# Moving early transfers, MLP steps, weight sums and transposes in a fused attention and MLP kernel

## The chip, the cores and the metric

The kernel runs on one core of one Trainium2 chip. Its time is the device time of one execution in microseconds (us). Three runs of the kernel before gave 350.06, 349.75 and 347.81 us, median 349.75.

## The reference

Eight batches of eight heads, 576 tokens, head size 64: forgetting attention, and then an MLP over all 4608 tokens.

```python
scores = q @ k.T / sqrt(64)
cum = cumsum(log(clip(f, 0.0001, 1.0)))
scores = where(causal, -1e9, scores + cum[i] - cum[j])
x = softmax(scores) @ v              # heads side by side: 4608 x 512
h = x @ w_in                         # 512 x 2048
out = (h - tanh(h)) @ w_out          # 2048 x 512, float32
```

## The kernel before, in words

**Slots.** The attention works on pairs of heads: four pairs in each batch, 32 pairs. Slot p makes the scores of pair p and the values (the product with v) of pair p - 1. From slot 5 on a slot is a list made by `att_items` (L559): seven score tiles, numbered 0 to 6 here. A tile is TensorE work (`scores`, L346), an exponential on ScalarE (L362) and a triangular select on GpSimd (L373). After tile 1 come `values` of the pair before (30 small matmuls on TensorE, L383, then three VectorE instructions up to L391) and `turn`, two transposing DMAs on SyncE's queue (L404, L406). For batches 0 to 2 a slot also transposes q and k of the next pair on TensorE (`trans`, L293; copied out by VectorE, L303, or in slots 7 and 8 by ScalarE, L301): behind tiles 0 and 3, in slot 5 behind tiles 2 and 4, in slots 7 and 9 behind tiles 1 and 4. The loads of later batches are hung on tiles too (`LOADS`); they follow the select of their tile in GpSimd's queue. The five loads of batch 2's v stand on tiles 2 to 6 of slot 6, the first loads of its q and k on tiles 1 to 4 of slot 5.

**MLP steps.** Between attention items a slot hands out `take` MLP steps. A block of 512 tokens has 30 steps: sixteen times `mlp1` (four matmuls, tanh on ScalarE, an addition on VectorE, L431), then fourteen half products with `w_out`, eight matmuls each. The products use Strassen's scheme, so they also need sums of the activations (`sums`, L445) and of the weights. Each quarter of the weight sums is made once, by two VectorE instructions (`wsum`, L275), which follow two neighbouring steps of block 0. With the steps counted from 0, slot 4 does steps 0 to 4; slots 5 to 8 take 6 each and slot 9 takes 7, so slot 9 ends with step 35. The products are, in this order: (1) steps 16, 17; (2) 18; (6) 19, 20; (2) 21; (5) 22, 23; (7) 24, 25; (3) 26, 27; (4) 28, 29. Product 6 needs weight sum 2, product 5 sum 0, product 7 sum 1, product 4 sum 3. Steps 21, 25, 27 and 29 close a quarter of the output and store it; two buffers `ost` hold what is being stored.

**Loads.** All loads of q, k, v and weights are issued by GpSimd, one after another, on one queue. Before, batch 0's v comes in seven DMAs: head 0, head 1, the last 64 tokens of all heads, then (after q and k of heads 6 and 7) four blocks of 128 tokens with heads 2 to 7. Batch 1, `w_in` and `w_out` follow, and batch 2's first q.

Of the kernel before, what the change touches and what calls it, by code (L numbers as in the profile page):

```python
# [17 lines left out]
FAR = 3  # L18
# [5 lines left out]
def kernel(  # L24
# [13 lines left out]
    B, H, S, D = q.shape  # L38
# [4 lines left out]
    NPAIR = H // 2  # L43
    NJ = 5
# [3 lines left out]
    NFT = DFF // P  # L48
# [31 lines left out]
    qn, kn = ([t[0:S // NT6, :].rearrange("p (h n d) -> p h n d", h=H, n=NT6) for t in raw] for raw in (qraw, kraw))  # L80
    qb, kb = ([t[:, 0:NJ * DM].rearrange("p (n e) -> p n e", n=NJ) for t in raw] for raw in (qraw, kraw))
    vn = [qkp.tile([P, NJ, H, VW], FP16, tag=f"vn{i}", name=f"vn{i}") for i in range(2)]
    QT = [qkp.tile([D + 3, H, S], FP16, tag=f"QT{i}", name=f"QT{i}") for i in range(2)]
    KT = [qkp.tile([D + 3, H, PITCH], FP16, tag=f"KT{i}", name=f"KT{i}") for i in range(2)]
# [3 lines left out]
    def load_qk(dst, src, b, h0, h1):  # L88
        nc.gpsimd.dma_start(
            out=dst[b % 2][:, h0:h1, :, :].rearrange("p h n d -> p (h n) d"),  # L90
            in_=src[b, h0:h1, :, :].rearrange("h s d -> (h s) d").rearrange("(m p) d -> p m d", p=S // NT6))
# [13 lines left out]
    def load_v_rest(b):  # L105
        nc.gpsimd.dma_start(out=vn[b % 2][0:S % P, NJ - 1, :, 0:D],
                            in_=v[b, :, S - S % P:S, :].rearrange("h p d -> p h d"))

    def load_v_head(b, h):
        nc.gpsimd.dma_start(out=vn[b % 2][:, 0:NJ - 1, h, 0:D],  # L110
                            in_=v[b, h, 0:S - S % P, :].rearrange("(n p) d -> p n d", p=P))

    def load_v_block(b, n, h0, h1):
        nc.gpsimd.dma_start(out=vn[b % 2][:, n, h0:h1, 0:D],  # L114
                            in_=v[b, h0:h1, n * P:(n + 1) * P, :].rearrange("h p d -> p h d"))

    def load_v(b):
        for n in range(NJ - 1):
            load_v_block(b, n, 0, H)
        load_v_rest(b)  # L120
# [63 lines left out]
    def cum_q():  # L184
        nc.scalar.activation(out=cq, in_=cum, func=AF.Copy, bias=-SHIFT * inv_qscale, scale=inv_qscale)

    load_v_head(0, 0)
    load_v_head(0, 1)
    load_v_rest(0)
    load_qk(qn, q, 0, 6, H)  # L190
    load_qk(kn, k, 0, 6, H)
    for n in range(NJ - 1):
        load_v_block(0, n, 2, H)

    def pads():
        nc.vector.scalar_tensor_tensor(out=pick[:, 2:3], in0=id16[:, 1:2], scalar=-1.0, in1=id16[:, NH + 1:NH + 2],
# [80 lines left out]
    def spin(n):  # L277
        t32 = ps_av.tile([P, 2, UW], FP32, tag="av", name="spin")
        for _ in range(n):
            nc.tensor.matmul(out=t32[:, 0, :], lhsT=ones16[:, 0:P], rhs=ones16[:, 0:UW])  # L280
# [7 lines left out]
    def trans(b, c, src, dst, engs):  # L288
        pn, g3 = S // NT6, NT6 // 2
        t16 = t_bank().bitcast(FP16)[:, 0:2 * S // 2].rearrange("p (a g n) -> p a g n", a=2, g=g3)  # L290
        for a in range(2):
            for g in range(g3):
                nc.tensor.transpose(out=t16[:, a, g, :], in_=src[b % 2][:, 2 * c + a, 2 * g:2 * g + 2, :],  # L293
                                    identity=id16[0:pn, 0:pn])
        for a0, an in ((0, 1), (1, 1)) if len(engs) > 2 else ((0, 2),):
            for e in range(2):
                h0 = 2 * c + a0
                to = dst[b % 2][0:D, h0:h0 + an, 0:S].rearrange("d a (g e p) -> d a g e p", g=g3, e=2)[:, :, :, e, :]
                of = t16[e * D:(e + 1) * D, a0:a0 + an, :, :]
                if engs[2 * a0 + e] == "A":  # L300
                    nc.scalar.activation(out=to, in_=of, func=AF.Copy)  # L301
                else:
                    nc.vector.tensor_copy(out=to, in_=of)  # L303
            if a0 == 0 and engs == "AAAA":
                cum_q()
# [70 lines left out]
    def values(b, c, a):  # L376
        if a == 0:
            av = ps_av.tile([P, 2, 512], FP32, tag="av", name="av")
            AV[(b, c)] = av[:, :, 0:NJ * (D + 1)].rearrange("p a (i d) -> p a i d", i=NJ)
        av = AV[(b, c)]  # L380
        for ib in range(NJ):
            for j in range(ib + 1):
                nc.tensor.matmul(out=av[:, a, ib, :], lhsT=E.pop((b, c, a, j, ib)),  # L383
                                 rhs=vn[b % 2][:, j, 2 * c + a, 0:D + 1], start=(j == 0), stop=(j == ib))
        if a == 0:
            return
        xn = XN[(b, c)] = fin.tile([P, NJ, P], FP16, tag="xn", name="xn")
        rs = fin.tile([P, 2, NJ, 1], FP32, tag="rs", name="rs")
        nc.vector.tensor_scalar_add(out=rs, in0=av[:, :, :, D:D + 1], scalar1=1e-9)  # L389
        nc.vector.reciprocal(out=rs, in_=rs)  # L390
        nc.vector.tensor_tensor(out=xn.rearrange("p i (a d) -> p a i d", a=2), in0=av[:, :, :, 0:D],  # L391
                                in1=rs.to_broadcast([P, 2, NJ, D]), op=ALU.mult)

    def turn(b, c):
        xn = XN.pop((b, c))
        r0 = b % 3 * S
        if b == 0:
            xt = t_bank().bitcast(FP16)[:, 0:S]
            for ib in (NJ - 1, 0, 1, 2, 3):
                w0 = min(ib * P, S - P)  # L400
                nc.tensor.transpose(out=xt[:, w0:w0 + P], in_=xn[:, ib, :], identity=id16)
            nc.vector.tensor_copy(out=XR[:, c, r0:r0 + S], in_=xt)
            return
        nc.sync.dma_start_transpose(out=XR[:, c, r0:r0 + S - D].rearrange("p (n t) -> p n t", t=P),  # L404
                                    in_=xn[:, 0:NJ - 1, :].rearrange("p n d -> p (n d)"))
        nc.sync.dma_start_transpose(out=XR[:, c, r0 + S - D:r0 + S], in_=xn[D:P, NJ - 1, :])  # L406
# [97 lines left out]
    for u in range(NU):  # L504
        mlp += [[(mlp1, u, ft)] for ft in (turns if u else turns[:10] + turns[12:14] + turns[10:12] + turns[14:])]
        mlp += [[(product, u, n, g)] for n, g in ((1, 0), (1, 1), (2, 0), (6, 0), (6, 1), (2, 1))]
        mlp += [[(product, u, n, g)] for n in (5, 7, 3, 4) for g in range(2)]
    for at, n in ((NFT - 2, 0), (NFT, 2), (NFT + 3, 1), (NFT + 6, 3)):
        for o in range(2):
            mlp[at + o] += [(wsum, n, o * K2 // 2, (o + 1) * K2 // 2)]  # L510

# [2 lines left out]
    def step():  # L514
        for fn, *args in mlp[STEPS[0]]:
            fn(*args)
        STEPS[0] += 1
# [7 lines left out]
    def first_slot(p):  # L525
        here = pairs[p]
        before = pairs[p - 1] if p else None
        for what in FIRST[p]:
# [27 lines left out]
            else:  # L556
                spin(int(what))

    def att_items(p):  # L559
        items = []  # L560
        before = pairs[p - 1]
        after = pairs[p + 1] if p + 1 < len(pairs) else None
        for ti in range(len(TILES)):
            if p < len(pairs):
                items.append((lambda ti=ti: scores(*pairs[p], (ti,), "late"), True))
            items += [(load, False) for load in LOADS.get((p, ti), ())]
            if after and after[0] < FAR and ti in ((1, 4) if p in (2 * NPAIR - 1, 2 * NPAIR + 1) else (2, 4) if p == NPAIR + 1 else (0, 3)):
                dst, src = (KT, kn) if ti > 2 else (QT, qn)
                items.append((lambda dst=dst, src=src: trans(*after, src, dst, "AA" if 2 * NPAIR - 1 <= p <= 2 * NPAIR else "VV"), True))
            if ti == 1:  # L570
                items += [(lambda a=a: values(*before, a), a == 1) for a in range(2)]
                items.append((lambda: turn(*before), True))
        return items

    with tc.manual_schedule(engines={PE, mybir.EngineType.Pool, mybir.EngineType.SP, mybir.EngineType.DVE,
                                     mybir.EngineType.Activation}):
        with tc.tile_pool(name="ps_t2", bufs=1, space=PSUM) as POOLS["t"]:
            with tc.tile_pool(name="ps_two", bufs=2, space=PSUM) as POOLS["s"]:
                for p in range(NPAIR):
                    first_slot(p)  # L580
        del POOLS["t"]
        POOLS["m"] = ctx.enter_context(tc.tile_pool(name="ps_m", bufs=3, space=PSUM))
        POOLS["s"] = ctx.enter_context(tc.tile_pool(name="ps_sc", bufs=2, space=PSUM))
        first_slot(NPAIR)
        for p in range(NPAIR + 1, len(pairs) + 1):
            items = att_items(p)
            take = 6 if p <= 2 * NPAIR else 7 if p == 2 * NPAIR + 1 or p % 2 == 0 else 8
            whole, given, n = sum(c for _, c in items), 0, 0
            for emit, counts in items:
                emit()  # L590
                n += counts
                while given < take and (given + 1) * whole <= n * take and STEPS[0] < len(mlp):
                    step()
                    given += 1
        while STEPS[0] < len(mlp):
            step()
# [28 lines left out]
```

## Time and profile before

| what | us |
|---|---|
| median of three runs | 349.75 |
| the profiled execution | 351.51 |
| its span | 349.7 |
| TensorE busy | 334.1 |
| VectorE busy | 253.0 |
| ScalarE busy | 220.4 |
| GpSimd busy | 179.3 |

The span runs from the first to the last instruction of the profiled execution. Busy time is the union of an engine's instructions; matmuls overlap each other, and a busy TensorE is not TensorE at its peak. "PEclk" is the granted clock of TensorE, 1.00 being full speed. An idle time of an engine counts only where that engine sets the end.

### The profile page before, as it was taken

How to read it: one execution, taken by the hardware profiler on the slowest of the kernel's cores; microseconds unless marked ns; L12 is line 12 of the kernel's file. 1: busy time of each engine (PE TensorE's matmuls, PEld its weight loads, DVE VectorE, ACT ScalarE, POOL GpSimd, SP SyncE). 2: the span in 40 equal slices, each digit the busy share in tenths (PEclk: the TensorE clock that was granted, in tenths of full speed). 3: DMA queues.
4: the chain of work that ended last, by engine and by line, in shares of the span. 5: the costliest groups of instructions: out<-in, count | busy, mean ns of one | idle time of the engine just before them, and what ended most of it. 6: DMA issues, size and time to landing. Idle time of an engine off the chain costs nothing.

```text
span 349.7 us, 8656 instructions
## 1 busy us (share of the span) xinstructions
PE 334.1 (96%) x3297; PEld 233.6 (67%) x3297; DVE 253.0 (72%) x521; ACT 220.4 (63%) x412; POOL 179.3 (51%) x327
## 2 busy tenths in 40 slices
PE   7889995997999999999999999999999999999996
PEld 2676564783568656887887568755887787477475
DVE  7686996628997489848884889378937873873872
ACT  6676873766765687568755875588558843623631
POOL 8996755484676736775567447752322220500500
PEclk9999997899999999999999999999999999999999
DMA  9999999999999997999699969994122004003003
GB/s 99 137 156 171 187 199 132 132 106 169 127 142 114 170 164 75 119 164 168 69 114 149 194 78 102 157 170 78 48 79 50 19 21 134 0 3 120 3 0 122
DMA packets 169592, 38.82 MB, mean 111 GB/s; under 512 B 155938, under 2 KB 169486, under 8 KB 169550
## 3 DMA queue, kind: packets, MB, share of 16 engines
q0 software_dynamic: 116608, 18.36, 83.9%
q1 hardware_dynamic: 52942, 19.90, 28.2%
q8 instruction: 26, 0.43, 0.5%
q14 instruction: 16, 0.13, 0.1%
HBM read 36.85 MB, written 9.44 MB: 132 GB/s over the span
## 4 chain that ended last, share of the span: by engine, by line
PE 81%; DMA 8%; DVE 6%; ACT 2%; SPq 1%; issue 1%; POOL 0%; DVEq 0%; POOLq 0%
PE mb L418 30%; PE px L466 16%; PE mb L466 14%; PE ps L346 11%; PE av L383 8%; DMA qn<-in_q_dram 6%; DMA out_dram<-ost 2%; DVE gt L431 1%; PE t L293 1%; DVE KT L303 1%; DMA ws<-in_f_dram 1%; ACT e L362 1%; DVE sm L445 1%; DVE xn L391 1%; ACT th L425 1%
## 5 line engine op out<-in xcount | busy, mean ns | idle before, releaser
L418 PE MATMUL mb<-XR,win 128*128 128x512 f16 (+4 forms) x704 | 141.3, 340 | 2.3 <-DVE gt L431 2.2
L362 ACT ACTIVATE e<-ps 128x512 f16<-128x512 f32 (+1 forms) x183 | 109.4, 618 | 23.5 <-PE ps L346 15.7
L425 ACT ACTIVATE th<-mb 128x512 f32<-128x512 f32 x144 | 86.5, 601 | 51.4 <-PE mb L418 45.8
L431 DVE TENSOR_TENSOR gt<-mb,th 128x512 f16<-128x512 f32 x144 | 97.4, 687 | 24.1 <-ACT th L425 22.7
L373 POOL TENSOR_SCALAR_AFFINE_SELECT e<-e 128x128 f16<-128x128 f16 x162 | 59.6, 372 | 99.3 <-ACT e L362 98.5
L418 PEld LDWEIGHTS <-win 128*128 128x128 f16 x704 | 61.7, 97 | 51.0 <-issue 4.4
L346 PE MATMUL ps<-QT,KT 67*128 67x448 f16 (+4 forms) x376 | 73.9, 279 | 3.1 <-DVE KT L303 1.9
L466 PEld LDWEIGHTS <-gt 128*128 128x128 f16 x576 | 54.1, 98 | 11.3 <-DVE gt L431 1.0
L346 PEld LDWEIGHTS <-KT 67*128 67x128 f16 x384 | 36.4, 98 | 25.9 <-DVE KT L303 3.8
L466 PEld LDWEIGHTS <-sm 128*128 128x128 f16 x432 | 40.9, 98 | 6.7
L496 DVE TENSOR_TENSOR ost<-mb,part 128x512 f32<-128x512 f32 x25 | 17.2, 686 | 28.2 <-PE mb L466 9.2
L466 PE MATMUL mb<-ws,gt 128*128 128x256 f16 x288 | 36.4, 272 | 0.0
L383 PEld LDWEIGHTS <-e 128*128 128x128 f16 x896 | 32.5, 98 | 3.4 <-DVE xn L391 0.6
L383 PE MATMUL av<-vn,e 128*128 128x65 f16 x896 | 34.3, 194 | 0.4 <-DVE xn L391 0.4
L483 ACT ACTIVATE part<-px 128x512 f32<-128x512 f32 x24 | 14.3, 597 | 30.2 <-PE px L466 30.2
L466 PE MATMUL px<-ws,sm 128*128 128x256 f16 x256 | 31.6, 272 | 0.0
L114 POOL DMA_DIRECT2D vn<-in_v_dram x32 | 28.4, 890 | 4.1 <-DMA wout<-in_moe_w_out_dram 2.4
L391 DVE TENSOR_TENSOR xn<-av,rs 128x640 f16<-128x640 f32 x32 | 26.4, 825 | 1.1
L389 DVE TENSOR_SCALAR rs<-av 128x10 f32<-128x10 f32 x32 | 5.2, 162 | 25.0 <-PE av L383 24.9
L445 POOL TENSOR_TENSOR sm<-gt 128x512 f16<-128x512 f16 x4 | 4.6, 1156 | 36.2 <-DVE gt L431 36.2
L95 POOL DMA_DIRECT2D qn<-in_q_dram x25 | 21.9, 875 | 1.5 <-issue 1.4
L466 PE MATMUL mb<-wout,gt 128*128 128x256 f16 x160 | 22.2, 280 | 0.0
(92 smaller groups left out, 320.4 us busy)
## 6 DMA issues: line engine op xcount, KB each, us to landing
out_dram<-ost SPq DMA_DIRECT2D x34, 256.0 KB
vn<-in_v_dram POOLq DMA_DIRECT2D x28, 128.0 KB, 5.8
qn<-in_q_dram POOLq DMA_DIRECT2D x20, 128.0 KB, 3.7
kn<-in_k_dram POOLq DMA_DIRECT2D x20, 128.0 KB, 4.3
win<-in_moe_w_in_dram POOLq DMA_DIRECT2D x4, 512.0 KB, 9.0
wout<-in_moe_w_out_dram POOLq DMA_DIRECT2D x2, 1024.0 KB, 17.1
qn<-in_q_dram POOLq DMA_DIRECT2D x10, 144.0 KB, 6.5
kn<-in_k_dram POOLq DMA_DIRECT2D x10, 144.0 KB, 6.8
```

Source lines behind the costliest of these rows:

```text
L95: nc.gpsimd.dma_start(out=dst[b % 2][0:pn, n, :].rearrange("p (h d) -> p h d", h=H), in_=src[b, :, n * P:n * P + pn, :].rearrange("h p d - ...
L114: nc.gpsimd.dma_start(out=vn[b % 2][:, n, h0:h1, 0:D], in_=v[b, h0:h1, n * P:(n + 1) * P, :].rearrange("h p d -> p h d"))
L346: nc.tensor.matmul(out=ps[:, col:col + n], lhsT=KT[b % 2][0:rows, h, j * P:(j + 1) * P], rhs=QT[b % 2][0:rows, h, i0:i0 + n], start=True, ...
L362: nc.scalar.activation(out=eb[:, :, lo:hi], in_=banks[:, 0:n2, lo:hi], func=AF.Exp, scale=qscale)
L373: nc.gpsimd.affine_select(out=view, in_=view, compare_op=ALU.is_ge, fill=0.0, base=0, pattern=pat, channel_multiplier=-1)
L383: nc.tensor.matmul(out=av[:, a, ib, :], lhsT=E.pop((b, c, a, j, ib)), rhs=vn[b % 2][:, j, 2 * c + a, 0:D + 1], start=(j == 0), stop=(j == ib))
L391: nc.vector.tensor_tensor(out=xn.rearrange("p i (a d) -> p a i d", a=2), in0=av[:, :, :, 0:D], in1=rs.to_broadcast([P, 2, NJ, D]), op=ALU. ...
L418: nc.tensor.matmul(out=hps[:, o:o + n], lhsT=win[:, ci, ft * P:(ft + 1) * P], rhs=XR[:, ci, t:t + n], start=(ci == 0), stop=(ci == NCH - 1))
L425: nc.scalar.activation(out=th, in_=hps, func=AF.Tanh, scale=-1.0)
L431: nc.vector.tensor_tensor(out=GT[(u, ft)], in0=hps, in1=th, op=ALU.add)
L466: nc.tensor.matmul(out=ps[:, g * E2:(g + 1) * E2], lhsT=left(k), rhs=right[:, k, :], start=(first and (g == 0 or last) and k == 0), stop=( ...
L496: nc.vector.tensor_tensor(out=ost, in0=ps, in1=PART.pop((u, {2: 1, 7: 5, 4: 6}[n])), op=ALU.add)
```

## The change

1. Batch 0's v is loaded by `load_v(0)`: four blocks of 128 tokens with all heads and the rest, all ahead of q and k of heads 6 and 7. That is five DMAs instead of seven.
2. Slots 5, 6 and 7 take 5 MLP steps instead of 6; slots 8 and 9 take 8 instead of 6 and 7. Slot 9 ends with step 35 as before.
3. Weight sum 2 follows steps 17 and 18 instead of 16 and 17, sum 1 steps 22 and 23 instead of 19 and 20, sum 3 steps 25 and 26 instead of 22 and 23. Sum 0 stays behind steps 14 and 15.
4. In slot 7 the transposes of q and k stand behind tiles 3 and 5 (the fourth and the sixth) instead of 1 and 4, and in slot 9 behind tiles 2 and 5 instead of 1 and 4.

```diff
-    load_v_head(0, 0)
-    load_v_head(0, 1)
-    load_v_rest(0)
+    load_v(0)
     load_qk(qn, q, 0, 6, H)
     load_qk(kn, k, 0, 6, H)
-    for n in range(NJ - 1):
-        load_v_block(0, n, 2, H)
...
-    for at, n in ((NFT - 2, 0), (NFT, 2), (NFT + 3, 1), (NFT + 6, 3)):
+    for at, n in ((NFT - 2, 0), (NFT + 1, 2), (NFT + 6, 1), (NFT + 9, 3)):
         for o in range(2):
             mlp[at + o] += [(wsum, n, o * K2 // 2, (o + 1) * K2 // 2)]
...
+    TURNED = {NPAIR + 1: (2, 4), 2 * NPAIR - 1: (3, 5), 2 * NPAIR + 1: (2, 5)}
+    TAKEN = {NPAIR + 1: 5, NPAIR + 2: 5, 2 * NPAIR - 1: 5, 2 * NPAIR: 8, 2 * NPAIR + 1: 8}
...
-            if after and after[0] < FAR and ti in ((1, 4) if p in (2 * NPAIR - 1, 2 * NPAIR + 1) else (2, 4) if p == NPAIR + 1 else (0, 3)):
-                dst, src = (KT, kn) if ti > 2 else (QT, qn)
+            if after and after[0] < FAR and ti in TURNED.get(p, (0, 3)):
+                dst, src = (KT, kn) if ti == TURNED.get(p, (0, 3))[1] else (QT, qn)
...
-            take = 6 if p <= 2 * NPAIR else 7 if p == 2 * NPAIR + 1 or p % 2 == 0 else 8
+            take = TAKEN.get(p, 7 + p % 2)
```

## The prediction

> **What bounds the kernel now.** I looked first at the busy times: TensorE is at 96% of the span, so time can be won or lost only where it idles or runs slowly. The table by slot (columns: stretch, then busy us of PE, PEld, DVE, ACT, POOL, then PEclk, DMA share, GB/s) says where, for slots 5 to 9:
>
> ```profile
> PE 334.1 (96%) x3297; PEld 233.6 (67%) x3297; DVE 253.0 (72%) x521; ACT 220.4 (63%) x412; POOL 179.3 (51%) x327
> ...
> 34.97:43.74 8.77, 8.32 (x79) 4.44 (x77) 8.39 (x19) 7.14 (x15) 6.27 (x12) 1.00 1.68 187
> 43.74:51.77 8.03, 8.03 (x82) 5.01 (x83) 7.24 (x15) 5.95 (x13) 4.28 (x10) 1.00 1.27 202
> 51.77:67.27 15.50, 11.38 (x104) 8.75 (x102) 10.13 (x21) 7.20 (x14) 6.75 (x12) 0.78 3.14 128
> 67.27:75.31 8.04, 8.04 (x102) 6.96 (x102) 4.16 (x8) 7.20 (x14) 7.10 (x13) 1.00 1.29 117
> 75.31:87.15 11.84, 9.48 (x88) 5.37 (x86) 6.99 (x15) 7.09 (x14) 7.01 (x14) 1.00 1.67 157
> ```
>
> Slots 6 and 8 are pure TensorE: 8.03 us with six steps. Slot 7 needs 15.50, slot 9 (seven steps) 11.84. The timeline of PE and of DVE and the granted clock explain both:
>
> ```profile
> 57.48 0.66 PE L293 MATMUL t<-id,qn 96*128 96x96 f16 x6 [4.07 <-DMA qn<-in_q_dram]
> 82.96 1.02 PE L418 MATMUL mb<-XR,win 128*128 128x512 f16 x4 [1.49 <-DVE gt L431]
> 87.15 0.39 PE L346 MATMUL ps<-QT,KT 67*128 67x512 f16 x1 [0.74 <-DVE KT L303]
> ...
> 79.48 0.69 DVE L496 TENSOR_TENSOR ost<-mb,part 128x512 f32<-128x512 f32 x1 [6.81 <-DMA out_dram<-ost]
> ...
> 56.00:57.00 1.00, 0.00 (x0) 0.00 (x0) 0.98 (x2) 0.00 (x0) 0.10 (x1) 0.83 3.12 138
> 57.00:58.00 1.00, 0.52 (x7) 0.52 (x8) 0.00 (x0) 0.00 (x0) 0.28 (x1) 0.50 3.63 130
> 60.00:63.00 3.00, 3.00 (x16) 2.06 (x14) 2.93 (x8) 0.60 (x1) 1.98 (x4) 0.50 3.02 137
> 63.00:64.00 1.00, 1.00 (x9) 0.72 (x8) 0.85 (x2) 0.28 (x2) 0.31 (x1) 0.75 4.26 107
> 64.00:65.00 1.00, 1.00 (x15) 0.90 (x13) 0.00 (x0) 0.78 (x3) 0.59 (x2) 1.00 4.56 118
> ```
>
> In slot 7 PE waits 4.07 us for batch 2's first q; the granted clock falls to 0.50 from about 56.7 to 63.5, so the 6.0 us from 57.48 to 63.5 do 3.0 us of work. In slot 9 VectorE stands 6.81 us for a store that holds an `ost` buffer, and PE loses 1.49 and 0.74 us behind it.
>
> GpSimd's queue comes next, since it issues that q and makes the selects:
>
> ```profile
> 7.78 1.54 POOL L110 DMA_DIRECT2D vn<-in_v_dram  x2
> 9.31 0.71 POOL L106 DMA_DIRECT2D vn<-in_v_dram  x1
> 11.73 3.31 POOL L114 DMA_DIRECT2D vn<-in_v_dram  x4
> ...
> 54.68 0.89 POOL L114 DMA_DIRECT2D vn<-in_v_dram  x1 [2.37 <-DMA wout<-in_moe_w_out_dram]
> 55.58 0.52 POOL L373 TENSOR_SCALAR_AFFINE_SELECT e<-e 128x256 f16<-128x256 f16 x1
> 57.72 0.69 POOL L106 DMA_DIRECT2D vn<-in_v_dram  x1 [1.62 <-DMA qn<-in_q_dram]
> ```
>
> The load of v at 54.68 (slot 6, tile 5) waited for the second half of `w_out`, the load eight places ahead of it; the one at 57.72 waited for batch 2's q, again eight ahead. So at most eight loads are under way, and the select of tile 6 of slot 6 (55.58 to 56.10) stands behind such a wait. Before the change nobody feels it: the values that need this tile come after the transposes at 57.48.
>
> **The change part by part.**
>
> Unit prices. The chain of work shows sixteen product matmuls, two steps, in 1.75 us, so a step is 0.875; a slot without steps is 8.03 - 6 x 0.875 = 2.78 (two transposes at 0.26, values 0.90, and 1.36 for the tiles, 0.215 for each but tile 3).
>
> ```profile
> 107.98 1.75 PE px L466 x16
> ...
> 88.88 0.90 PE av L383 x30
> ...
> 92.66 0.26 PE t L293 x6
> ```
>
> *v in whole blocks.* GpSimd's issue of batch 0's v falls from 1.54 + 0.71 + 3.31 = 5.56 us to 4 x 0.89 + 0.71 = 4.27: every later early load is issued 1.29 us sooner. Whether it lands sooner depends on the queue of transfers. The next rows give the time from issue to landing of a load issued at 11.7, of the last one of that stretch (15.9), of the second half of `w_out` (34.9), and of batch 2's first k (40.3) and first q:
>
> ```profile
> L114 POOL DMA_DIRECT2D vn<-in_v_dram x1: 837/837/837, 11.7 to 11.7; - x1
> DMA to landing us min/median/max: 4.4/4.4/4.4
> ...
> L89 POOL DMA_DIRECT2D kn<-in_k_dram x1: 935/935/935, 15.9 to 15.9; - x1
> DMA to landing us min/median/max: 5.3/5.3/5.3
> ...
> L218 POOL DMA_DIRECT2D wout<-in_moe_w_out_dram x1: 888/888/888, 34.9 to 34.9; - x1
> DMA to landing us min/median/max: 19.5/19.5/19.5
> ...
> L89 POOL DMA_DIRECT2D kn<-in_k_dram x1: 877/877/877, 40.3 to 40.3; - x1
> DMA to landing us min/median/max: 18.2/18.2/18.2
> ...
> 37.33 20.10 DMA qn<-in_q_dram
> ...
> 12.00:21.00 9.00, 7.86 (x140) 6.47 (x141) 5.19 (x12) 6.95 (x10) 8.94 (x12) 1.00 1.88 130
> ```
>
> The backlog at 16 us is under 1 us (5.3 against 4.4) and POOL is 8.94 of 9 us busy: issue is the limit there. Later the landing takes 19.5 us: transfers are the limit. A lead won in the first stretch is kept. The bounds are 0 and 1.29; I take 1.0, nearer the issue-bound row. On the other side, heads 6 and 7 of q and k are issued 4.27 - (1.54 + 0.71) = 2.0 us later, and the first values need all of v. Even a delay of 0 to 0.5 us of PE there costs nothing: it is covered by the wait in slot 7, and would cost in full without it.
>
> *Fewer steps, later transposes (slots 5 to 7).* PE leaves slot 5 0.9 to 1.0 us sooner and slot 6 again, reaching slot 7 at about 49.8. There tiles 0 and 1 (0.43) and then the values come, now ahead of the transposes. Two thirds of them (0.6) can run, until 50.8; the rest needs the select of tile 6 of slot 6, behind the v load that waits for `w_out`. That load starts at 54.68 - 1.0 = 53.7; add 0.89 and 0.52: 55.1. So the wait for q (landing 1.0 sooner too, at 56.4 instead of 57.4, when PE still has two steps to do) is gone, and a wait of 4.3 us for a select stands in its place, of the same length as the 4.07 before. I let the clock fall as it did, 3.0 us.
>
> *Sums later.* Sum 2 is queued on VectorE just ahead of product 6. With PE at half clock it is in time; at full clock PE would wait about 0.8 us at step 19. Sum 1 now follows steps 22 and 23, and step 24 needs it at once. Rows of VectorE (mean ns):
>
> ```profile
> L391 DVE TENSOR_TENSOR xn<-av,rs 128x640 f16<-128x640 f32 x5 | 4.1, 825 | 0.2
> L275 DVE TENSOR_TENSOR ws<-wout 128x1024 f16<-128x1024 f16 x4 | 2.9, 734 | 0.0
> L445 DVE TENSOR_TENSOR sm<-gt,sm 128x512 f16<-128x512 f16 x4 | 1.8, 468 | 0.0
> L496 DVE TENSOR_TENSOR ost<-mb,part 128x512 f32<-128x512 f32 x3 | 2.1, 692 | 9.9 <-DMA out_dram<-ost 6.8 <-PE mb L466 2.4 <-PE ps L346 0.8
> ```
>
> After step 21 VectorE has `ost` 0.69, a sum 0.47, the values' 1.25 (0.83 and two small ones), a sum 0.47, half of sum 1 0.73, a sum 0.47, the other half 0.73: 4.8 us. PE comes to the second half of step 24's matmuls after values 0.9, steps 22 and 23 1.75, tiles 2 and 3 0.28, and 0.4: 3.3. It waits 1.6 us with the pipeline's delay. Bounds: 0 if VectorE is ahead, 2.4 if it starts with a backlog. Sum 3 is done before step 28.
>
> *Eight steps in slots 8 and 9.* The chain's row of a store, and VectorE's copies of k:
>
> ```profile
> 73.87 5.49 DMA out_dram<-ost
> ...
> L303 DVE COPY KT<-t 64x576 f16<-64x576 f16 x7 | 3.2, 452 | 0.1
> ```
>
> The second store is now issued a slot boundary before the last `ost` needs its buffer: from step 25 PE still has steps 26 to 29, values and four tiles, 5.3 us, against 0.69 of `ost` and 5.49 of the transfer: VectorE may wait about 1 us for the buffer, with TensorE's banks filled ahead. So the 1.49 us goes. The late transposes of slot 9 (tile 5, with two steps behind) leave VectorE's copy of k late for slot 10 again: 0.85 us where it was 0.74. Bounds 0 and 1.8 (both halves of both copies).
>
> *Sum.* PE work from 55.1 to slot 10: slot 7, 2.78 + 5 x 0.875 - 0.43 - 0.6 = 6.12; slots 8 and 9, 9.78 each; 25.7. With 3.0 + 1.6 + 0.85 slot 10 starts at 86.25 instead of 87.15: 0.9 us sooner. Behind it the program is the same and bound by PE. The profiled execution took 351.51 us, 1.76 over the median shown; against the median the forecast is 349.75 - 0.9 = 348.9.
>
> [...] The trace shows one fall of the clock, after 3.3 us without a matmul, and shallower gaps without one (0.74 and 1.49). [...]
>
> **The rivals.**
> [...]
> - *The select comes later (slower).* Place: GpSimd's v load in slot 6. Batch 2's q landed 3.0 us after `w_out` (57.4 against 54.4), while k landed 1.1 us behind q (58.5), so some 1.9 us of the queue went to other transfers, such as the transposing DMAs of slot 6. These are issued sooner now; if their 1.9 us falls ahead of `w_out`'s end, all is 1.9 later: 350.8; if v brings no lead either, 351.8. It decides from 0.9 us on, that is if `w_out` lands after 54.3.
> - *VectorE keeps up.* No wait at step 24 and slot 10: 2.45 less, 346.4. For it: VectorE was busy for only 4.16 us in slot 8.
> - *The order does nothing*: the old waits return in new places to the same sum, within a microsecond of 349.75; this is inside the first forecast's own range, 347.5 to 350.3.
>
> **How the numbers follow.** Forecast 0.42; clock stays up 0.25; select later 0.18; VectorE keeps up 0.15. One per cent, 3.5 us, is about what a measurement can tell from no change: below 346.25 is faster. Half of the second and most of the fourth case, where they go together (344.3) surely, give 0.28; slower (over 353.25) only where the third adds to a fallen clock that lasts longer, 0.10; same 0.62. The range is 345.0 to 351.4: it cuts the joint case and the worst of the third.
>
> **What would show it.** In PE's timeline of slot 7 a wait of about 4 us at the values (released by POOL's select), none at the transposes; 0.50 of the clock behind it; a wait of 1 to 2 us in slot 8 at the products with the third weight sum; no long wait of VectorE for a store; `w_out`'s second half about 1 us sooner. The forecast is wrong if the values do not wait for the select, if `w_out` does not move, or if step 24 does not wait.

## The result, and the profile after

Twenty runs of the changed kernel have a median of 347.76 us, twenty of the kernel before 350.42; the ratio, taken from the means, is 0.9944, with a 95% interval of 0.9923 to 0.9966. (One run of the changed kernel, 692 us, is left out of all comparisons.) So the change gains 0.6% (2.0 us) by the means and 2.7 us by the medians, where 0.9 us was forecast. By its interval that is inside the 1% that the prediction called the same, and the time is 1.1 us under its number.

The profiled execution of the changed kernel spans 345.9 us, against 349.7. The table by slot, slots 5 to 9 (columns as before: stretch, busy us of PE, PEld, DVE, ACT, POOL, PEclk, DMA share, GB/s):

```profile
PE 331.7 (96%) x3297; PEld 232.2 (67%) x3297; DVE 252.7 (73%) x521; ACT 219.9 (64%) x412; POOL 178.0 (51%) x325
...
35.83:44.16 8.33, 7.40 (x75) 4.13 (x74) 7.81 (x18) 5.84 (x13) 5.10 (x9) 1.00 1.51 194
44.16:51.32 7.16, 7.16 (x76) 4.24 (x75) 6.31 (x13) 5.78 (x13) 3.74 (x9) 1.00 1.39 196
51.32:61.36 10.04, 8.08 (x92) 5.96 (x91) 8.79 (x18) 7.51 (x15) 8.24 (x14) 1.00 2.77 144
61.36:72.40 11.04, 10.11 (x121) 8.58 (x119) 6.66 (x14) 7.56 (x14) 6.67 (x11) 1.00 1.77 141
72.40:83.42 11.02, 9.89 (x96) 6.08 (x94) 7.05 (x16) 7.28 (x14) 7.17 (x15) 1.00 1.64 141
```

Slot 10 begins at 83.42 instead of 87.15, and that difference of 3.7 us is all but 0.1 us of the difference of the spans. Slot 7 takes 10.04 us instead of 15.50, and its clock is 1.00 instead of 0.78. PE's timeline has these waits from slot 5 up to slot 10, and ahead of them the longest one of slots 1 to 4 (the first row, in slot 1). The row at 56.57 is the transposes of q in slot 7. Line numbers of the changed kernel are 4 lower from the changed loads on:

```profile
16.64 0.31 PE L379 MATMUL av<-vn,e 128*128 128x65 f16 x5 [0.93 <-DMA vn<-in_v_dram]
41.71 0.42 PE L289 MATMUL t<-id,kn 96*128 96x96 f16 x6 [0.93 <-DVE QT L299]
52.92 0.27 PE L379 MATMUL av<-vn,e 128*128 128x65 f16 x3 [0.22 <-POOL e L369]
54.24 0.45 PE L379 MATMUL av<-vn,e 128*128 128x65 f16 x9 [1.05 <-POOL e L369]
56.57 0.42 PE L289 MATMUL t<-id,qn 96*128 96x96 f16 x6
60.92 0.60 PE L462 MATMUL mb<-ws,sm 128*128 128x256 f16 x4 [0.53 <-DVE ws L271]
67.28 0.60 PE L462 MATMUL mb<-ws,gt 128*128 128x256 f16 x4 [0.38 <-DVE ws L271]
68.42 0.60 PE L462 MATMUL mb<-ws,gt 128*128 128x256 f16 x4 [0.55 <-DVE ws L271]
83.42 0.39 PE L342 MATMUL ps<-QT,KT 67*128 67x512 f16 x1 [1.13 <-DVE KT L299]
```

The wait for q in slot 7 is gone (the row at 56.57 has none). The values wait ahead of it, 0.22 us for one select and 1.05 us for that of the late tile, 1.27 in all. GpSimd's timeline, and the time from issue to landing of the two `w_out` loads (issued at 31.9 and 32.8), show why that is short:

```profile
52.41 0.46 POOL L369 TENSOR_SCALAR_AFFINE_SELECT e<-e 128x128 f16<-128x128 f16 x1
52.83 0.89 POOL L114 DMA_DIRECT2D vn<-in_v_dram  x1
53.73 0.45 POOL L369 TENSOR_SCALAR_AFFINE_SELECT e<-e 128x256 f16<-128x256 f16 x1
...
L214 POOL DMA_DIRECT2D wout<-in_moe_w_out_dram x2: 890/894/898, 31.9 to 32.8; - x2
DMA to landing us min/median/max: 14.1/16.3/18.6
```

`w_out`'s second half landed at 32.8 + 18.6 = 51.4 instead of 54.4, before GpSimd came to the v load, which went out without a wait. The late tile was held up only by the 0.89 us of issuing that load. The clock did not fall.

**One execution is not the median.** In the profiles the clock falls to 0.50 for stretches of 3.41 us. One of them goes with a mean granted clock of 0.995 over the execution (`old_turns`, 54.46 to 57.87), two with 0.990 (the kernel before, 56.67 to 63.50), three with 0.985 (`no_v`, 14.56 to 24.80). Sorted by this mean, with the kernel before as it ran beside the experiments below (63 executions, since its twenty runs above have no clock on record):

| mean granted clock | before: executions, median us | changed: executions, median us |
|---|---|---|
| 0.998 to 1.000 | 5, 347.78 | 14, 347.70 |
| 0.994 or 0.995 | 30, 349.50 | 4, 348.94 |
| 0.991 or less | 28, 350.98 | 1, 350.32 |

The changed kernel's executions mostly keep the full clock (14 of 19), the old kernel's seldom do (5 of 63). That the medians of the first row are equal does not yet mean that nothing else was gained: five of 63 are a selected group, in which the wait of slot 7 may have been shorter. The experiment with added matmuls, below, gives the kernel before at full clock without that choice: 348.65.

### The profile page after: what moved, and what is told of

Its sections match the earlier page's. It is cut to its first block, busy times and chain, and to the rows that moved or that the text cites. A ratio compares the mean times of both kernels' runs of the same rounds, so it can differ in the third digit from the quotient of the medians.

```text
span 345.9 us, 8654 instructions
## 1 busy us (share of the span) xinstructions
PE 331.7 (96%) x3297; PEld 232.2 (67%) x3297; DVE 252.7 (73%) x521; ACT 219.9 (64%) x412; POOL 178.0 (51%) x325
## 4 chain that ended last, share of the span: by engine, by line
PE 85%; DVE 4%; DMA 3%; POOL 3%; ACT 2%; issue 1%; POOLq 0%; ACTq 0%
PE mb L414 33%; PE px L462 16%; PE mb L462 14%; PE ps L342 12%; PE av L379 8%; DMA KT<-cc 2%; DMA vn<-in_v_dram 2%; POOL vn L114 1%; ACT e L358 1%; DVE gt L427 1%; PE t L289 1%; DVE sm L441 1%; POOL kn L89 1%; ACT th L421 1%; DVE KT L299 1%
## 5 line engine op out<-in xcount | busy, mean ns | idle before, releaser
L95 POOL DMA_DIRECT2D kn<-in_k_dram x25 | 21.4, 854 | 1.7 <-issue 1.6
```

Source lines behind the costliest of these rows:

```text
L95: nc.gpsimd.dma_start(out=dst[b % 2][0:pn, n, :].rearrange("p (h d) -> p h d", h=H), in_=src[b, :, n * P:n * P + pn, :].rearrange("h p d - ...
```

## The experiments

Each was compared with runs of the kernel before on the same chip; "at full clock" are the executions with a mean of 0.998 or more. The experiments ran on three chips. On these the kernel before with one stretch at half clock has medians of 349.50, 349.46 and 349.83, so times at full clock can be set against each other to about 0.4 us. On which chip the changed kernel ran is not on record.

**Whole blocks of v alone** (`v_only`): the kernel before with `load_v(0)` in place of the seven loads, as in the first hunk of the diff.

> The kernel before with batch 0's v in whole blocks and nothing else. Theory (the lead of the early loads is what pays): the second half of w_out lands some 3 us sooner, as in the changed kernel (51.4 instead of 54.4), batch 2's q at 52.5 to 54.4, and PE, which comes to the transposes of slot 7 at about 54.3 (0.9 us of its own lost in slots 0 to 4), waits under 1 us. The clock stays at 1.00. The wait for the store in slot 9 stays (about 2.2 us of PE). Time 344 to 346, so this part alone would beat the whole change. Rival (the moved steps and transposes are what pays): the landings move by under 1 us, PE waits 3 us or more in slot 7, the clock falls, 349.5 to 351.

Measured: 346.59 us, ratio 0.9932 (0.9900 to 0.9963); 8 of 12 at full clock, median 346.38 there. PE's waits from slot 7 on:

```profile
54.03 0.43 PE L289 MATMUL t<-id,qn 96*128 96x96 f16 x6 [0.15 <-DMA qn<-in_q_dram]
57.51 0.60 PE L462 MATMUL mb<-ws,sm 128*128 128x256 f16 x4 [0.41 <-DVE ws L271]
75.00 1.02 PE L414 MATMUL mb<-XR,win 128*128 128x512 f16 x4 [0.42 <-DVE ost L492]
77.73 1.02 PE L414 MATMUL mb<-XR,win 128*128 128x512 f16 x4 [1.50 <-DVE gt L427]
81.92 0.39 PE L342 MATMUL ps<-QT,KT 67*128 67x512 f16 x1 [0.74 <-DVE KT L299]
```

The wait for q is 0.15 us, the store's wait in slot 9 stays (0.42 + 1.50). The theory stands, half a microsecond optimistic, but the clock did not stay up in all executions: 4 of 12 fell. One of the four parts does the work of the whole change. Whether it does it better depends on how one compares: at full clock it is 1.3 us ahead (346.38 against 347.70), and by the ratios the two are not told apart.

**The change without that part** (`no_v`): the first hunk undone.

> The changed kernel with batch 0's v in its old seven loads. Theory: w_out's second half lands at 54 again, the select of tile 6 of slot 6 comes at about 56, the values of slot 7 wait 4 to 5 us for it (1.3 in the changed kernel), and the clock falls in most executions: 350 to 353. Rival: the values wait about as in the changed kernel and the time is 347.5 to 348.5.

Measured: 351.63, ratio 1.0052 (1.0024 to 1.0079); none of 12 at full clock. The other three parts together make the kernel slower. The profiled execution does not show the expected place, though: in it the clock fell to 0.50 already in the early slots, from 14.56 to 24.80, PE came to slot 7 some 3.5 us late, and the wait for the select was 1.27 us as in the changed kernel:

```profile
56.51 0.27 PE L383 MATMUL av<-vn,e 128*128 128x65 f16 x3 [0.22 <-POOL e L373]
57.82 0.45 PE L383 MATMUL av<-vn,e 128*128 128x65 f16 x9 [1.05 <-POOL e L373]
```

So the total agrees with the theory, and the trace does not show its mechanism. This execution, with a mean clock of 0.985, is also the only one of the twelve under 0.990; in which slots the clock of the others fell is not known.

**The old places of the sums** (`old_sums`):

```diff
-    for at, n in ((NFT - 2, 0), (NFT + 1, 2), (NFT + 6, 1), (NFT + 9, 3)):
+    for at, n in ((NFT - 2, 0), (NFT, 2), (NFT + 3, 1), (NFT + 6, 3)):
```

> The changed kernel with the weight sums in their old places. Theory: the waits of PE for a weight sum at step 19 (0.5 us) and step 24 (0.9 us) go and nothing else moves: 346.3 to 347.0. Rival (the sums stood in VectorE's way in slots 6 and 7, and moving them is part of the gain): the later copies of slot 7 come later, 348 or more.

Measured: 347.02, ratio 0.9941 (0.9904 to 0.9978); 6 of 12 at full clock, median 346.22, which is 1.5 us under the changed kernel's 347.70. The waits at step 24 are gone, and the one at step 19 is 0.19:

```profile
63.08 0.60 PE L462 MATMUL mb<-ws,sm 128*128 128x256 f16 x4 [0.19 <-DVE ws L271]
```

At full clock the later sums cost what their waits show. Over all executions the two are not told apart (0.9941 here, 0.9944 for the whole change), and this version lost clock more often, in 6 of 12 executions against 5 of 19.

**Matmuls on constants in the old wait** (`before_spin`). The added matmuls are no part of the computation.

```diff
             items += [(load, False) for load in LOADS.get((p, ti), ())]
+            if p == 2 * NPAIR - 1 and ti == 1:
+                items.append((lambda: spin(16), False))
```

> The kernel before with 16 matmuls on constants (3.5 us, their result is never read) ahead of the transposes of q in slot 7, where PE waits 4.07 us. Theory (the fall of the clock costs 3 us and comes from that idle stretch): the clock stays at 1.00 in all executions, and the time is 347.3 to 348.5, 2 to 3 us under the kernel before, with no other work moved. Rival (the half clock costs little, since slot 7 waits for other engines there anyway): within 1 us of the kernel before.

Measured: 348.75, ratio 0.9978 (0.9948 to 1.0009): by the interval not told apart from the kernel before. Still, 10 of 12 executions are at full clock (5 of 63 without the matmuls), so with the idle stretch of 4.07 us filled the clock mostly stays up. They take 348.65 there, 0.9 more than the five of the kernel before, which speaks for the selection named above. So of the 2.7 us between the two kernels' medians, the clock accounts for 1.0 (349.78 to 348.75, the medians of this comparison) to 1.8 (350.42 to 348.65), and shorter waits, 348.65 against 347.70, for about 1.0. This split is an estimate across runs whose own difference is not clear of noise. The theory was right on the cause of the fall, and put the gain too high. In the profile the added matmuls end before q lands, and PE still waits:

```profile
52.86 3.62 PE L280 MATMUL spin<-ones 128*128 128x512 f16 x16
57.45 0.43 PE L293 MATMUL t<-id,qn 96*128 96x96 f16 x6 [0.97 <-DMA qn<-in_q_dram]
```

**The last two v loads of batch 2 later** (`loads_later`):

```diff
-            at_tile(p0, 16 + n if b == 2 else 7 + n + late, lambda b=b, n=n: load_v_part(b, n))
+            at_tile(p0, 16 + n + 3 * (n > 2) if b == 2 else 7 + n + late, lambda b=b, n=n: load_v_part(b, n))
```

> The changed kernel with the last two loads of batch 2's v hung three tiles later (tiles 1 and 2 of slot 7), so that the select of tile 6 of slot 6 no longer stands behind one. Theory (the select behind the load is what the values of slot 7 wait for): that wait falls from 1.27 us to 0.5 or less; executions at full clock take 346.7 to 347.2 instead of 347.7. Rival (the values wait for the late tile itself, its scores and exponential): the wait and the time stay.

Measured: 347.14, ratio 0.9902 (0.9876 to 0.9928); 6 of 6 at full clock, 347.13. The wait for the select is one of 0.22:

```profile
52.83 0.81 PE L379 MATMUL av<-vn,e 128*128 128x65 f16 x12 [0.22 <-POOL e L369]
```

This holds although `w_out` landed only at 53.4 in this profile: with the loads behind it, the select no longer depends on that.

**The same without the lead of v** (`no_v_loads_later`): both edits on the changed kernel.

> The changed kernel with batch 0's v in its old seven loads and the two loads of batch 2's v hung later. Without the lead of the early loads the clock fell in every execution. Theory (it fell because the values waited 4 us or more for a select behind a load that waited for w_out): with the select free the wait is under 1.5 us, most executions keep the full clock, median 347.5 to 349. Rival (the old loads themselves bring the fall, in slots 0 to 4): the clock is at 0.99 or below in most executions and the time stays at 350.5 to 352.

Measured: 349.50, ratio 0.9967 (0.9943 to 0.9991); 5 of 12 at full clock, 347.96. Better than `no_v` by 2 us, as the theory has it, but not by as much as expected. The select was free and another wait, which I had not counted, took over: q landed at 57.4, late as in the kernel before. PE's row, and the clock after it:

```profile
57.40 0.43 PE L293 MATMUL t<-id,qn 96*128 96x96 f16 x6 [2.75 <-DMA qn<-in_q_dram]
...
54.82:58.23 3.41, 0.83 (x12) 0.77 (x13) 3.34 (x8) 0.51 (x2) 2.02 (x3) 1.00 3.31 117
58.23:61.64 3.41, 3.41 (x20) 2.24 (x18) 1.11 (x4) 2.50 (x5) 3.41 (x7) 0.50 2.49 130
```

**The old counts of steps** (`old_take`):

```diff
-    TAKEN = {NPAIR + 1: 5, NPAIR + 2: 5, 2 * NPAIR - 1: 5, 2 * NPAIR: 8, 2 * NPAIR + 1: 8}
+    TAKEN = {NPAIR + 1: 6, NPAIR + 2: 6, 2 * NPAIR - 1: 6, 2 * NPAIR: 6, 2 * NPAIR + 1: 7}
```

> The changed kernel with 6, 6, 6, 6 and 7 steps in slots 5 to 9. Theory: slot 7 begins 1.8 us later, so the values no longer wait for the select (1.3 us less), but the last store of block 0 comes sooner behind the second one and VectorE waits for its buffer again, up to 2 us of PE; full clock in most executions, 347.5 to 348.7 there. Rival (fewer steps early are what keeps the clock up): the clock falls in most executions, 350 or more.

Measured: 348.11, ratio 0.9922 (0.9891 to 0.9953). At full clock 347.44, a little under what the theory said; but only 2 of 7 executions are there, so the rival has part of the truth. The profiled execution is the slowest of the seven (351.32, mean clock 0.985). In it the store's wait is back (VectorE 5.2 us), and the last sum before product 6 is late by 1.05 + 1.50:

```profile
60.08 0.61 PE L462 MATMUL mb<-ws,sm 128*128 128x256 f16 x4 [1.05 <-DVE ws L271]
62.20 0.68 PE L462 MATMUL mb<-ws,sm 128*128 128x256 f16 x4 [1.50 <-DVE ws L271]
...
80.01 0.69 DVE L492 TENSOR_TENSOR ost<-mb,part 128x512 f32<-128x512 f32 x1 [5.20 <-DMA out_dram<-ost]
```

**The old places of the transposes** (`old_turns`):

```diff
-    TURNED = {NPAIR + 1: (2, 4), 2 * NPAIR - 1: (3, 5), 2 * NPAIR + 1: (2, 5)}
+    TURNED = {NPAIR + 1: (2, 4), 2 * NPAIR - 1: (1, 4), 2 * NPAIR + 1: (1, 4)}
```

> The changed kernel with the transposes of slots 7 and 9 behind tiles 1 and 4 again. Theory: q lands at 52.5, PE comes to the transposes of slot 7 at 52 and waits about 0.5 us, and the select has come when it reaches the values, so that the waits of slot 7 sum to 1 us or less; in slot 9 k is copied two steps sooner and the wait of 1.1 us ahead of slot 10 goes: executions at full clock 346.3 to 347.2. Rival (the later place of the transposes is part of the gain): PE waits 3 us or more for q, the clock falls, 349 or more.

Measured: 347.84, ratio 0.9910 (0.9878 to 0.9942). Both sides are half right. At full clock it takes 346.18, 1.5 us less than the changed kernel and a little under the theory's range (two executions only), and the wait ahead of slot 10 is gone. But PE waits 2.41 us for q (it landed at 54.0, not 52.5), and 4 of 6 executions lose one stretch of the clock:

```profile
53.98 0.43 PE L289 MATMUL t<-id,qn 96*128 96x96 f16 x6 [2.41 <-DMA qn<-in_q_dram]
...
51.05:54.46 3.41, 0.89 (x10) 0.47 (x9) 2.10 (x5) 1.57 (x5) 2.65 (x5) 1.00 2.08 155
54.46:57.87 3.41, 3.41 (x37) 2.45 (x36) 1.19 (x3) 1.88 (x3) 2.84 (x5) 0.50 3.31 137
```

The later place in slot 7 buys safety from the landing of q; the later place in slot 9 costs 1.1 us.

**Old sums and later loads together** (`sums_loads`): the edits of `old_sums` and `loads_later`.

> The changed kernel with the weight sums in their old places and the two loads of batch 2's v hung three tiles later. Theory (waits of PE add up where the clock stays): 0.5 + 0.9 us of waits for sums and 0.5 to 1 us of the wait for the select go; executions at full clock 345.4 to 346.0. Rival (the sums of the old places come into the way again): 346.2 or more, as with the old sums alone.

Measured: 346.04, ratio 0.9888 (0.9865 to 0.9911); 6 of 6 at full clock. Between the two expectations. The sums' waits are gone, but VectorE now waits 1.69 us for the store and PE 0.60 behind it, so part of the gain was given back there:

```profile
75.63 1.02 PE L414 MATMUL mb<-XR,win 128*128 128x512 f16 x4 [0.60 <-DVE ost L492]
81.29 0.39 PE L342 MATMUL ps<-QT,KT 67*128 67x512 f16 x1 [1.13 <-DVE KT L299]
...
74.89 0.69 DVE L492 TENSOR_TENSOR ost<-mb,part 128x512 f32<-128x512 f32 x1 [1.69 <-DMA out_dram<-ost]
```

**Whole blocks and a third store buffer** (`v_ost3`): `v_only` and

```diff
     tmp = ctx.enter_context(tc.tile_pool(name="tmp", bufs=2))
+    osp = ctx.enter_context(tc.tile_pool(name="osp", bufs=3))
...
-        ost = tmp.tile([P, DM], FP32, tag="th" if half == 0 and n == 4 else "ost", name="ost") if half != 1 else PART.pop((u, n, "ost"))
+        ost = (tmp if half == 0 and n == 4 else osp).tile([P, DM], FP32, tag="th" if half == 0 and n == 4 else "ost", name="ost") if half != 1 else PART.pop((u, n, "ost"))
```

> The kernel before with batch 0's v in whole blocks and three buffers instead of two for the output quarters being stored. Theory (VectorE's wait for a store buffer in slot 9 costs PE 1.9 us): that wait goes; executions at full clock 344.4 to 345.0 against 346.4 with whole blocks alone. Rival (behind the store VectorE is late anyway): 346 or more.

Measured: 344.60, ratio 0.9852 (0.9826 to 0.9878), the best version; 5 of 6 at full clock. VectorE takes the last quarter when PE has it, not when a store ends:

```profile
71.85 0.69 DVE L493 TENSOR_TENSOR ost<-mb,part 128x512 f32<-128x512 f32 x1 [4.29 <-PE mb L463]
...
80.28 0.39 PE L343 MATMUL ps<-QT,KT 67*128 67x512 f16 x1 [0.74 <-DVE KT L300]
```

**Old sums, later loads, and slot 9's transposes in the old place** (`best1`): `sums_loads` and `2 * NPAIR + 1: (1, 4)` in `TURNED`.

> The changed kernel with the old sums, the two loads of batch 2's v hung later, and slot 9's transposes behind tiles 1 and 4 again (slot 7's stay behind 3 and 5). Theory: besides the waits for sums and select, the 1.13 us ahead of slot 10 goes; executions at full clock 344.3 to 345.0, and most executions are at full clock, since no wait in slot 7 is over 1 us. Rival: the copies of slot 9 then wait behind the store and the gain at slot 10 is lost, 345.4 or more.

Measured: 345.77, ratio 0.9875 (0.9844 to 0.9906), all at full clock. The wait ahead of slot 10 is gone in its profile, yet the median is only 0.3 under `sums_loads`, and the six executions lie between 343.46 and 346.76. The expectation failed. The time is the rival's, but not by the rival's mechanism: VectorE waits for no store in slot 9. The profile shows where a part goes. Slot 10 begins at 79.72, 1.57 us sooner than in `sums_loads` (81.29), while the span is only 0.8 us shorter (343.7 against 344.5). So about 0.8 us is lost again behind slot 10, some 0.5 of it in waits of PE for VectorE's `gt` (1.0 us in all against 0.5). The first row is the start of slot 10, the others are two waits that `sums_loads` does not have:

```profile
79.72 0.38 PE L342 MATMUL ps<-QT,KT 67*128 67x512 f16 x1
95.97 0.28 PE L462 MATMUL mb<-wout,gt 128*128 128x256 f16 x1 [0.21 <-DVE gt L427]
96.57 0.28 PE L462 MATMUL mb<-wout,gt 128*128 128x256 f16 x1 [0.32 <-DVE gt L427]
```

Why the six executions scatter was not settled.

## Why the prediction was right or wrong

**Right in direction and within its range, by another case than the likeliest.** The forecast was 348.9 with the clock falling as before. What came was the case in which the clock stays up, given 0.25 by the author's estimate, with no run behind it; by the forecast's terms it is 348.9 - 3.0 + 0.8 = 346.7. Measured is 347.76. That the number is only 1.1 us off the forecast is luck in part: the 3.0 us charged for the clock did not come in most executions, and the forecast stood on three runs of the kernel before (median 349.75), where twenty gave 350.42.

- *The values wait for the select behind a load.* Right as a mechanism: the release by POOL is in the profile, the wait for q is gone, and hanging the loads later takes the wait away (`loads_later`). Wrong in size: 1.27 us in place of 4.3. The late tile's select ended at 54.2 instead of 55.1, 0.9 us sooner, and PE came to it at 53.2 instead of 50.8, 2.4 us later. Two terms of that step were mis-sized. The lead of `w_out` was put at 1.0 with an upper bound of 1.29, GpSimd's saved issue time; it is 3.0 in this profile. And PE reached slot 7 at 51.3, not 49.8, for it lost 0.93 us in slot 1 waiting for v (0 to 0.5 was allowed) and 0.93 in slot 5 waiting for a copy of q, which had been no term at all. So the wait was short mainly because PE came late to it, which the change had not been meant to do: that the clock stayed up is luck in part.
- *The lead.* The bound was the error. In the four kernels with the old loads the second half of `w_out` landed at 52.9 to 54.6, in the nine with whole blocks at 51.4 to 53.4; the means differ by 2.0 us, more than the saved issue time. The time from issue to landing hardly differs: it is 18.8 to 19.5 us with the old loads and 18.6 to 19.6 with whole blocks. Nearly all of the lead is there when GpSimd issues this load, at 34.1 to 35.3 and at 32.2 to 34.1, on average 1.75 us sooner. In the two profiles above it grows from 1.37 us at the first loads of `w_in` (16.75 and 15.38) to 2.1 us at `w_out` (34.9 and 32.8), with GpSimd's waits for earlier loads in between:

```profile
16.75 1.56 POOL L214 DMA_DIRECT2D win<-in_moe_w_in_dram  x2
25.31 0.70 POOL L106 DMA_DIRECT2D vn<-in_v_dram  x1 [0.49 <-DMA win<-in_moe_w_in_dram]
28.73 0.76 POOL L214 DMA_DIRECT2D win<-in_moe_w_in_dram  x1 [2.73 <-DMA win<-in_moe_w_in_dram]
...
15.38 1.58 POOL L210 DMA_DIRECT2D win<-in_moe_w_in_dram  x2
25.94 0.77 POOL L210 DMA_DIRECT2D win<-in_moe_w_in_dram  x1 [1.80 <-DMA win<-in_moe_w_in_dram]
27.69 0.89 POOL L89 DMA_DIRECT2D qn<-in_q_dram  x1 [0.98 <-DMA qn<-in_q_dram]
```

  The first three rows are the kernel before (3.22 us of waits), the last three the changed one (2.78). The prediction counted the saved issue time, and not that GpSimd would also wait less for earlier loads.
- *The clock, 3.0 us.* This step failed, and it is the one that decided. The prediction let the clock fall because the new wait was to be as long as the old. With 1.27 us it did not, and 14 of 19 executions kept it. Nor did every fall have so idle a stretch ahead of it as that of the kernel before, where PE was busy for 0.16 of 3.42 us (53.25 to 56.67): the clock fell after stretches of 3.41 us in which PE was busy for 0.83 (`no_v_loads_later`) and 0.89 (`old_turns`), and in `no_v` after this one, where PE was busy for 2.34:

```profile
11.15:14.56 3.41, 2.34 (x26) 1.45 (x26) 1.73 (x4) 2.21 (x5) 3.41 (x5) 1.00 2.02 123
14.56:17.97 3.41, 3.41 (x34) 2.51 (x33) 0.91 (x2) 1.69 (x2) 3.41 (x5) 0.50 1.98 131
```

- *The sums.* Right in place, less in size: 0.53 us at step 19 (0.8 expected at full clock) and 0.38 + 0.55 = 0.93 at step 24 (1.6 expected; the delay behind a sum, 0.1 of it, was 0.05: the sum ended at 68.37, the product began at 68.42). `old_sums` gains 1.5 us at full clock, the sum of the three.
- *The store and slot 10.* Right: VectorE has no wait for a store, and the copy of k is late by 1.13 (0.85 expected). `old_turns` and `v_ost3` confirm each.
- *The sum.* Slot 10 was put at 86.25; with the clock up, the prediction's own terms give 86.25 - 3.0 + 0.8 = 84.05, and measured is 83.42: the select came 0.9 us sooner, and the other terms, too high and too low, cost 0.3 more. Behind slot 10 the two profiles take the same time, 262.5 us, as the prediction had it.
- *Against the median.* The step from one profiled execution to the median was unsound. The profile of before had two stretches at half clock; by their mean clocks 30 of its 63 executions had one, and 5 none. The terms other than the clock, which the prediction put at 0.9 us of gain, came to about 1.0 by the added matmuls, and to 0.1 by the five executions at full clock; which of the two is nearer was not settled.

Still open: what of the early falls of the clock (`no_v`, `old_sums` and `old_take` had them in slots 1 to 3) belongs to the order of the first loads.

## What to carry to other kernels

Read a trace's granted clock together with its waits: in `old_turns`, behind an idle stretch of 2.41 us of TensorE, the clock stood at half for 3.41 us, of which half, another 1.7 us, is an estimate of the loss. Whether it falls varies from one execution to the next (4 of 6 lost that stretch), so sort the runs by clock before putting a gain down to an edit. When an operation is moved ahead of a wait, ask what the wait had been hiding, here a select queued behind a load on the same engine. And test the parts of a composite change alone: here one part carried the gain, and without it the others were no gain at all (ratio 1.0052).

## What the runs showed of the hardware

- The clock stayed at half for 3.41 us (`old_turns`), 6.8 us (the kernel before) or 10.24 us (`no_v`), which is one, two or three steps of 3.41 us, and identical programs differ in it: the kernel before ran with mean clocks from 0.984 to 1.000, and with the first and the second stretch of 3.41 us at half clock its median rises by about 1.6 us each (347.78, 349.50, 350.98, the wait ahead of the fall included).
- The busy share of TensorE in a stretch of 3.41 us did not decide alone. The clock fell after 2.34 of 3.41 us busy in `no_v`, and stayed up after 1.92 of 3.41 in slot 9 of the kernel before:

```profile
80.57:83.98 3.41, 1.92 (x13) 0.83 (x11) 3.18 (x7) 1.52 (x4) 2.39 (x4) 1.00 1.47 156
```

  The first stretch holds 26 matmuls, the second 13; whether that is the reason was not tried.
- 1.29 us less of issue time on GpSimd's queue (batch 0's v takes 3.55 + 0.72 = 4.27 us, 5.56 before) grew on the way. In the two profiles above the second half of `w_out` went out 2.1 us sooner and landed 3.0 us sooner. Over all profiles its landing moved by 2.0 us on average.
